# Where weights and first-batch folds of a Fourier + two-MoE kernel are prepared: ahead of the first step, or within the steps

## The chip, the cores and the metric

One NeuronCore of a Trainium2 chip runs the whole program. The metric is device time in microseconds (us); lower is better. Engines are named TensorE (PE, with its weight loads as PEld), VectorE (DVE), ScalarE (ACT), GpSimd (POOL) and SyncE (SP, which here only issues transfers).

## The reference

```python
X = np.fft.fft(np.fft.fft(x, axis=1), axis=2).real     # x: 8 x 3072 x 256
x = X.reshape(24576, 256)
g = x @ w_gate; val = x @ w_val                        # 256 x 1536 each
x = (g * sigmoid(g) * val) @ w_out                     # 1536 x 256
logits = x @ m2_gate                                   # 256 x 8, routing with capacity 3072 per expert
out[mask_e] = relu(x[mask_e] @ w1[e]) @ w2[e]          # for each expert e
```

The inputs are float32, except the three weights of the first MoE: they are float64, and the kernel narrows their 64-bit words to float32 itself.

## The kernel before

The program has two phases. `phase1` computes the real part of the 2-D FFT and the first MoE; `phase2` routes tokens and runs the second MoE. The change is in `phase1` only.

**Tiles and steps.** `phase1` works on 48 tiles of 512 tokens (6 tiles for each of 8 batches). A tile has 12 steps, one for each 128 columns of the hidden layer (`NF` = 12), so there are 576 steps `g`. One step does, in this order of the program (lines 674 to 702): `advance(2g)`, the side work of slot A(g); `products(g, 1)` into bank Q, which ScalarE copies to `qs`; `products(g, 0)` into a bank Pp; ScalarE's rounding `hi` and GpSimd's remainder `lo` of step g-2; `columns(g)`, four VectorE operations; ScalarE's Silu and VectorE's `hidden(g-1)`; `out_proj(g-3)`, 12 TensorE products into four Y banks; `advance(2g+1)`, the side work of slot Z(g). The order is written out by hand: an engine runs its instructions in the order of the program, and waits where one needs another engine's result.

**Side work.** `at(s, gen)` puts a generator into slot s. Every `advance` takes one piece (up to the next `yield`) from each generator in its slot and moves it on to the next slot, so a generator with four pieces runs through four half-steps.

**What is prepared.** The transform along the 3072 axis uses cosine and sine tables on TensorE; before it, `fold` adds and subtracts the four mirrored parts of an x tile (five elementwise operations) into `z0` to `z5`, six folds for a batch. The transform along 256 is folded into the weights: `narrow` turns 64-bit words into float32 on VectorE (four operations, and one ScalarE mask), and `fold_w` multiplies a 512-column block of w_gate or w_val by the cd or sd table on TensorE, from where ScalarE takes the rounded part, and for sd also a row that goes to HBM and comes back as `w2`, and VectorE the remainder (line 214). There are three blocks `j`, each good for four steps of a tile: block 0 for columns 0 to 3, and so on. `prep_wo(c)` narrows two row blocks of w_out, transposes them on TensorE (line 240), rounds them (ScalarE line 243, GpSimd line 244), and multiplies the transposed blocks with `m2g` (line 248), which gives the eight logit columns that `prep_wl` appends to all six pairs (lines 254, 255). `fft_t` transforms column 128 for all batches in six parts; its result goes to HBM (`tscr`) and comes back, broadcast, as `tb`, one row for each tile. `fft_half` transforms a tile, sine and cosine half; it needs `tb`, the ce and se tables, and all six `z`.

**The start of phase 1** (lines 518 to 629) is straight code up to step 0. All loads go through SP's queue in the order written: W block 0, cd and sd, the column-128 data, m2g, x tiles 0 and 1, w_out in two groups with x tiles 2 and 3 in between, x tile 4, later x tile 5, ce, se, W blocks 1 and 2. VectorE narrows block 0; folds 0, 2, 4 run on GpSimd and 1, 3, 5 on VectorE; the six `prep_wo` are interleaved with them, using Y banks; then come the column-128 part, the two half transforms of tile 0, and the narrowing of block 1. Within the steps, `prep_units(1)` starts in slot Z(0), `prep_block(2)` in A(1), with bank F (one buffer) for block 2's products. The later parts for column 128 and tile 1's half transforms use bank F as well.

Of the kernel before, what the change touches and what calls it, by code (L numbers as in the profile page):

```python
# [86 lines left out]
def phase1(ctx, tc, io, yscr, Lall, ident, idt, NT, choice=None):  # L87
# [142 lines left out]
    def prep_wo(c, pl):  # L230
# [6 lines left out]
        pp = bank("Y", 4).rearrange("p (c t f) -> p c t f", c=2, t=2)  # L237
# [7 lines left out]
        yield  # L245
        for i in range(2):
            for t in range(2):
                nc.tensor.matmul(pl[:, E * (c + i) : E * (c + i) + E], woT[:, i, t, :], m2g[:, t, :], start=(t == 0), stop=(t == 1))
        yield

    def prep_wl(pl):
        for j, w in Wo.items():
            v = pl[:, 2 * E * j : 2 * E * j + 2 * E].rearrange("p (c e) -> p c e", c=2)
            nc.scalar.copy(w[:, :, 0, D:EXT], v)
            nc.vector.tensor_sub(w[:, :, 1, D:EXT], v, w[:, :, 0, D:EXT].bitcast(F32))
# [276 lines left out]
    load_x0(0)  # L532
    load_x0(1)
    for c in (0, 2, 4):
        load_wo(c)
    load_x0(2)
    load_x0(3)
    for c in (6, 8, 10):
        load_wo(c)
    load_x0(4)  # L540
    sp0 = fold_special(0, nc.vector, (("z5", 2), ("z4", 2)))
    next(sp0)

    for gv in range(2):
        narrow_w(0, gv)
    fw = [fold_w(0, gv, cs, "Y", 4) for gv in range(2) for cs in range(2)]
    for x in fw:
        next(x)
    vt = (("hi", 3), ("lo", 3))
    pl = bank("Pp", 2)  # L550
    pw = [prep_wo(c, pl) for c in range(0, NF, 2)]
    run(fold(0, 0, x0[0], nc.gpsimd), fold(0, 1, x0[1], nc.vector, vt))
    next(pw[0])
    for x in fw[0:2]:
        next(x)
    next(pw[1])
    for x in fw[2:4]:
        next(x)
    next(pw[0])
    x0.append(load_x(0, 5))  # L560
    load_tab("ce")
    load_tab("se")
    load_w(1)
    load_w(2)
    fold_t(xt, tsp)
    fp = [fold(0, i, x0[i], nc.gpsimd) for i in (2, 4)]
    fv = [fold(0, i, x0[i], nc.vector, vt) for i in (3, 5)]
    f2 = iter([x for i in (0, 1) for _ in range(10) for x in (fp[i], fv[i])])

    def some(n):  # L570
        for _ in range(n):
            next(next(f2))

    tt = fft_t(0, 0)
    for k in range(2, 8):
        some(8 if k < 7 else 0)
        if k < 6:
            next(pw[k])
        if k < 7:
            next(pw[k - 1])  # L580
        next(pw[k - 2])
        if k == 3:
            next(tt)
# [726 lines left out]
```

## Time and profile before

| | before |
|---|---|
| time, median of 3 (lowest, highest) | 3226.61 us (3226.33, 3227.45) |
| profiled execution, own time | 3226.93 us |
| its span | 3225.2 us |
| TensorE busy | 3100.4 us (96%) |
| VectorE busy | 2568.9 us (80%) |
| GpSimd busy | 1642.6 us (51%) |
| ScalarE busy | 1530.9 us (47%) |
| HBM read, written | 88.67 MB, 51.18 MB |

Busy time is the union of an engine's instructions; "xN" merges N alike instructions in a row. The granted clock (PEclk) is TensorE's, as a part of 2.4 GHz. "idle ... <-" names what ended an engine's idle time before an instruction.

### The profile page before, as it was taken

How to read it: one execution, taken by the hardware profiler on the slowest of the kernel's cores; microseconds unless marked ns; L12 is line 12 of the kernel's file. 1: busy time of each engine (PE TensorE's matmuls, PEld its weight loads, DVE VectorE, ACT ScalarE, POOL GpSimd, SP SyncE). 2: the span in 40 equal slices, each digit the busy share in tenths (PEclk: the TensorE clock that was granted, in tenths of full speed). 3: DMA queues.
4: the chain of work that ended last, by engine and by line, in shares of the span. 5: the costliest groups of instructions: out<-in, count | busy, mean ns of one | idle time of the engine just before them, and what ended most of it. 6: DMA issues, size and time to landing. Idle time of an engine off the chain costs nothing. (4 is left out here: it accounts for less than half of the span.)

```text
span 3225.2 us, 63210 instructions
## 1 busy us (share of the span) xinstructions
PE 3100.4 (96%) x23835; PEld 2927.4 (91%) x23835; DVE 2568.9 (80%) x5678; ACT 1530.9 (47%) x3034; POOL 1642.6 (51%) x1761
## 2 busy tenths in 40 slices
PE   6999999999999999999999985989999999999998
PEld 4899999999999999999999984868888888888998
DVE  8899999999999999999998887776767676765322
ACT  3555565565555555555565552233333333333332
POOL 3474674664764855846744443343434343434442
PEclk7999999999999999999999996989999999999999
DMA  5110100100100101101000001112121212112111
GB/s 208 31 38 20 44 31 32 44 25 24 51 20 31 51 18 38 38 18 46 31 25 11 18 34 43 42 61 68 41 69 42 69 42 73 41 67 70 51 44 37
DMA packets 71441, 143.94 MB, mean 45 GB/s; under 512 B 13602, under 2 KB 47442, under 8 KB 69088
## 3 DMA queue, kind: packets, MB, share of 16 engines
q1 hardware_dynamic: 50388, 71.96, 6.8%
q0 software_dynamic: 20736, 67.92, 6.4%
q8 instruction: 189, 3.10, 0.4%
q14 instruction: 116, 0.95, 0.1%
q10 hardware_dynamic: 12, 0.01, 0.0%
HBM read 88.67 MB, written 51.18 MB: 43 GB/s over the span
## 5 line engine op out<-in xcount | busy, mean ns | idle before, releaser
L688 POOL TENSOR_TENSOR lo<-hh,hi 128x512 fp32r<-128x512 f32 x576 | 745.2, 1294 | 752.4 <-ACT hi L687 739.6
L412 PE MATMUL Y<-Wo,hi 128*128 128x264 f32 x4608 | 866.5, 285 | 0.1
L412 PEld LDWEIGHTS Y<-Wo,hi 128*128 128x128 f32 x4608 | 710.2, 188 | 0.3 <-ACT hi L687 0.3
L412 PE MATMUL Y<-Wo,lo 128*128 128x264 f32 x2304 | 654.6, 284 | 5.2 <-POOL lo L688 5.2
L681 ACT COPY qs<-Q 128x512 f32<-128x512 f32 x576 | 340.0, 590 | 520.7 <-PE Q L381 511.0
L392 DVE SCALAR_TENSOR_TENSOR T<-tb,w,Q 128x256 f32<-128x256 f32 x1152 | 500.5, 475 | 97.9 <-ACT qs L681 91.3
L1141 PE MATMUL B<-w,hh 128*128 128x256 f32 x3072 | 577.2, 287 | 0.2 <-ACT hh L1121 0.2
L1150 POOL DMA_INDIRECT out_dram<-ot,id x192 | 192.5, 1003 | 585.1 <-ACT ot L1148 453.8
L1115 PE MATMUL A<-yh,w 128*128 128x512 f32 x1536 | 490.2, 400 | 0.1
L1141 PEld LDWEIGHTS B<-w,hh 128*128 128x128 f32 x3072 | 473.7, 189 | 3.3 <-ACT hh L1121 0.3
L400 DVE TENSOR_TENSOR hh<-sl,G 128x512 f32<-128x512 f32 x576 | 475.3, 825 | 1.1 <-issue 1.1
L381 PE MATMUL Q<-xh,W 128*128 128x256 f32 x2304 | 446.3, 286 | 14.4 <-DVE T L392 7.9
L412 PEld LDWEIGHTS Y<-Wo,lo 128*128 128x128 f32 x2304 | 434.1, 188 | 7.6 <-POOL lo L688 7.6
L1141 PE MATMUL B<-w,hl 128*128 128x256 f32 x1536 | 431.7, 281 | 0.2 <-DVE hl L1132 0.2
L381 PE MATMUL Pp<-xh,W 128*128 128x256 f32 x2304 | 431.2, 280 | 0.0
L687 ACT CAST hi<-hh 128x512 fp32r<-128x512 f32 x576 | 360.5, 626 | 70.8 <-DVE hh L400 66.1
L1132 DVE SCALAR_TENSOR_TENSOR hl<-A,hh 128x512 fp32r<-128x512 f32 x384 | 263.2, 687 | 163.4 <-ACT hh L1121 140.8
L393 DVE TENSOR_TENSOR G<-Pp,qs 128x512 f32<-128x512 f32 x576 | 392.2, 681 | 0.0
L394 DVE TENSOR_TENSOR G<-T,Pp 128x512 f32<-128x512 f32 x576 | 389.0, 675 | 0.0
L381 PEld LDWEIGHTS Q<-xh,W 128*128 128x128 f32 x2304 | 353.4, 188 | 27.1 <-ACT hi L687 14.4
L1121 ACT ACTIVATE hh<-A 128x512 fp32r<-128x512 f32 x384 | 229.3, 597 | 309.1 <-PE A L1115 256.5
L695 ACT ACTIVATE sl<-G 128x512 f32<-128x512 f32 x576 | 365.3, 634 | 0.0
(252 smaller groups left out, 5100.5 us busy)
## 6 DMA issues: line engine op xcount, KB each, us to landing
xs<-in_x_dram SPq DMA_DIRECT2D x43, 512.0 KB
yscr<-ys SPq DMA_DIRECT2D x40, 528.0 KB
tb<-tscr SPq DMA_DIRECT2D x48, 128.0 KB
raw<-in_wg_dram SPq DMA_DIRECT2D x6, 512.0 KB
raw<-in_wv_dram SPq DMA_DIRECT2D x6, 512.0 KB
rawWo<-in_wo_dram SPq DMA_DIRECT2D x12, 256.0 KB
yg<-yscr,idx POOLq DMA_INDIRECT x192
out_dram<-ot,id POOLq DMA_INDIRECT x192
```

The costliest lines, as they stand in the source:

```text
L381: nc.tensor.matmul(pp[:, gv * 256 : gv * 256 + 256], W[:, cs, gv, a, cc : cc + P], RI[t][cs][d], start=(i == 0), stop=(i == 2))
L392: nc.vector.scalar_tensor_tensor(T[:, gv, :], tb, w2[:, gv, c : c + 1], pq[:, gv * 256 : gv * 256 + 256], op0=ALU.mult, op1=ALU.add)
L393: nc.vector.tensor_sub(G[:, 0, :], pp, qs)
L394: nc.vector.tensor_add(rev(G[:, 1, :])[:, :, ::-1], T, rev(pp))
L400: nc.vector.tensor_mul(hh, s["sl"], s["G"][:, :, 256:512])
L412: nc.tensor.matmul(Yp[t][u], h[a][:, u * P : (u + 1) * P], Wo[c // 2][:, c % 2, d, :], start=(c == 0 and i == 0), stop=(c == NF - 1 and i ...
L681: nc.scalar.copy(s["qs"], s["pq"])
L687: nc.scalar.copy(hi, s["hh"])
L688: nc.gpsimd.tensor_sub(lo, s["hh"], hi.bitcast(F32))
L695: nc.scalar.activation(s["sl"], s["G"][:, :, 0:256], AF.Silu)
L1115: nc.tensor.matmul(pa, w[:, a, c : c + P], res["y", i][d][:, k, :], start=(n == 0), stop=(n == 5))
L1141: nc.tensor.matmul(pb[:, 0:D], h[a][:, s * P : (s + 1) * P], w[:, d, (f % 2) * D : (f % 2) * D + D], start=(n == 0), stop=(n == 23))
```

## The change

Four things. Loads: x tiles 0 to 5 come ahead of ce and se, and w_out and W blocks 1 and 2 behind them; x tile 5 is staged in the `ys` buffer. Ahead of step 0 only W block 0 is prepared, and all six folds run on VectorE. `prep_wo` takes bank F for its transposes and for its logit product, and appends its own pair's logit columns; `prep_wl` is gone. Block 1's narrowing goes into slots Z(0) and A(1), block 2 starts in A(2), and w_out pair c in A(c + 1), c = 0, 2, ..., 10.

```diff
-    def prep_wo(c, pl):
+    def prep_wo(c):
...
-        pp = bank("Y", 4).rearrange("p (c t f) -> p c t f", c=2, t=2)
+        pp = bank("F", 1).rearrange("p (c t f) -> p c t f", c=2, t=2)
...
         yield
+        pl = bank("F", 1)
         for i in range(2):
             for t in range(2):
-                nc.tensor.matmul(pl[:, E * (c + i) : E * (c + i) + E], woT[:, i, t, :], m2g[:, t, :], start=(t == 0), stop=(t == 1))
-        yield
-
-    def prep_wl(pl):
-        for j, w in Wo.items():
...
+                nc.tensor.matmul(pl[:, E * i : E * i + E], woT[:, i, t, :], m2g[:, t, :], start=(t == 0), stop=(t == 1))
+        yield
+        v = pl[:, 0 : 2 * E].rearrange("p (c e) -> p c e", c=2)
+        nc.scalar.copy(w[:, :, 0, D:EXT], v)
+        nc.vector.tensor_sub(w[:, :, 1, D:EXT], v, w[:, :, 0, D:EXT].bitcast(F32))
+        yield
...
-    load_x0(0)
-    load_x0(1)
-    for c in (0, 2, 4):
-        load_wo(c)
...
+    for i in range(5):
+        load_x0(i)
     sp0 = fold_special(0, nc.vector, (("z5", 2), ("z4", 2)))
     next(sp0)
+    x0.append(work.tile([P, 4, EXT], F32, tag="ys", bufs=1, name="x0")[:, :, 0:D])
+    nc.sync.dma_start(x0[5], io["x"][0, 5].rearrange("p (m d) -> p m d", m=4))
+    load_tab("ce")
+    load_tab("se")
+    load_wo(0)
+    load_w(1)
+    for c in range(2, NF, 2):
+        load_wo(c)
+    load_w(2)
 
     for gv in range(2):
         narrow_w(0, gv)
+    fold_t(xt, tsp)
     fw = [fold_w(0, gv, cs, "Y", 4) for gv in range(2) for cs in range(2)]
+    tt = fft_t(0, 0)
     for x in fw:
         next(x)
...
+    for x in fw:
         next(x)
...
-    for k in range(2, 8):
-        some(8 if k < 7 else 0)
...
+    for i in range(6):
+        run(fold(0, i, x0[i], nc.vector))
+        if i == 2:
             next(tt)
-        if k == 4:
+        if i == 3:
             next(tt)
             load_w2(0)
             tb0, r0 = load_tb(0), {}
...
-    prep_wl(pl)
...
-    narrow_w(1, 0)
     RI[0] = (r0[False], r0[True], tb0)
-    narrow_w(1, 1)
...
-    def prep_block(j):
+    def prep_block(j, *banks):
 
         for gv in range(2):
             narrow_w(j, gv)
             yield
-            if gv == 0:
+            if gv == 0 and j == 2:
                 yield
-        yield from prep_units(j, "F", 1)
+        yield from prep_units(j, *banks)
...
-    at(Z(0), prep_units(1, "Y", 4))
-    at(A(1), prep_block(2))
+    at(Z(0), prep_block(1, "Y", 4))
+    at(A(2), prep_block(2, "F", 1))
+    for c in range(0, NF, 2):
+        at(A(c + 1), prep_wo(c))
```

## Rows read from the trace of the kernel before

**Rows 1.** Busy time by stretch: stretch and length, busy (instructions) per engine, PEclk, DMA share, GB/s.

```profile
5.87:63.39 57.52, 34.28 (x129) 26.08 (x129) 48.83 (x83) 18.37 (x40) 26.70 (x22) 0.67 0.77 276
63.39:129.92 66.53, 58.41 (x362) 47.01 (x363) 58.26 (x112) 33.88 (x63) 14.92 (x13) 0.92 0.08 16
30.00:60.00 30.00, 19.64 (x92) 18.02 (x92) 24.21 (x42) 7.93 (x20) 15.94 (x13) 0.50 0.68 245
200.00:400.00 200.00, 198.92 (x1664) 197.82 (x1663) 185.97 (x352) 118.49 (x233) 119.15 (x109) 1.00 0.09 29
```

**Rows 2.** Timeline of TensorE, steps 0 and 13: start, duration, instruction, idle before it.

```profile
63.39 0.50 PE L381 MATMUL Q<-xh,W 128*128 128x256 f32 x2 [1.80 <-ACT xh L366]
...
129.92 0.39 PE L381 MATMUL Q<-xh,W 128*128 128x256 f32 x2
```

**Rows 3.** Timeline of VectorE: folds and narrowings of w_out ahead of step 0.

```profile
15.37 0.68 DVE L120 TENSOR_TENSOR fa<-x 128x512 f32<-128x512 f32 x1
...
22.50 0.69 DVE L178 SCALAR_TENSOR_TENSOR wo<-wm,wo 128x512 f32<-128x512 f32 x1
...
35.70 0.42 DVE L127 TENSOR_TENSOR fb<-fa 128x256 f32<-128x256 f32 x1
36.15 0.42 DVE L131 TENSOR_TENSOR z<-fb 128x256 f32<-128x256 f32 x1
36.74 0.43 DVE L172 TENSOR_SCALAR wo<-rawWo 128x512 int32<-128x512 int32 x1 [0.17 <-issue]
...
38.73 1.57 DVE L178 SCALAR_TENSOR_TENSOR wo<-wm,wo 128x512 f32<-128x512 f32 x1
```

**Rows 4.** Timeline: the last weight product of block 0 and a ScalarE read.

```profile
18.82 1.88 PE L207 MATMUL Y<-wt,sd 128*128 128x512 f32 x4
...
21.21 0.58 ACT L212 ACTIVATE row<-Y 1x512 f32<-1x512 f32 x1
```

**Rows 5.** Timeline: first half transform's weight loads, and VectorE's use of tb.

```profile
56.06 1.41 PEld L321 LDWEIGHTS Y<-ce,z 128*128 128x128 f32 x6
...
62.61 0.28 DVE L362 TENSOR_SCALAR ab<-tb 1x256 f32<-1x256 f32 x1
```

**Rows 6.** Busy time by stretch, at the end of the bulk and behind it.

```profile
43.00:44.00 1.00, 1.00 (x6) 1.00 (x6) 0.93 (x3) 1.00 (x4) 0.05 (x1) 0.50 0.63 254
...
49.00:51.00 2.00, 0.04 (x1) 0.00 (x0) 1.86 (x3) 0.00 (x0) 2.00 (x2) 0.50 0.47 71
```

**Rows 7.** Timeline: issues of SP's queue, and GpSimd's first fold, which waited for x.

```profile
9.77 0.82 SPq L531 DMA_DIRECT2D x<-in_x_dram  x2
...
13.42 3.77 POOL L120 TENSOR_TENSOR fa<-x 128x512 f32<-128x512 f32 x1 [11.86 <-DMA x<-in_x_dram]
...
46.83 0.29 SPq L294 DMA_DIRECT2D tscr<-tt  x1
...
48.54 0.44 SPq L336 DMA_DIRECT2D tb<-tscr  x1
```

**Rows 8.** Timeline of VectorE: narrowing of block 1 (two halves), and columns of step 0.

```profile
63.71 0.76 DVE L172 TENSOR_SCALAR wt<-raw 128x512 int32<-128x512 int32 x2
...
72.46 0.87 DVE L392 SCALAR_TENSOR_TENSOR T<-tb,w,Q 128x256 f32<-128x256 f32 x2
...
73.85 0.68 DVE L394 TENSOR_TENSOR G<-T,Pp 128x512 f32<-128x512 f32 x1
```

**Rows 9.** Timeline: TensorE's preparation work, and a weight remainder on VectorE.

```profile
35.93 1.09 PE L240 MATMUL Y<-ident,wo 128*128 128x128 f32 x4 [5.20 <-DVE wo L178]
36.81 1.72 PE L248 MATMUL Pp<-m2g,woT 128*128 128x8 f32 x8
...
67.62 3.73 PE L207 MATMUL Y<-wt,cd 128*128 128x512 f32 x4 [1.68 <-DVE wt L178]
...
74.31 0.38 PE L326 MATMUL F<-alt,tz 128*8 128x128 f32 x2
...
107.87 0.69 DVE L214 TENSOR_TENSOR W<-F,W 128x512 fp32r<-128x512 f32 x1 [1.69 <-ACT row L212]
```

More of the change, by code (lines that the diff above doesn't have):

```diff
@@ L245, in prep_wo @@
         yield
+        pl = bank("F", 1)
         for i in range(2):
             for t in range(2):
-                nc.tensor.matmul(pl[:, E * (c + i) : E * (c + i) + E], woT[:, i, t, :], m2g[:, t, :], start=(t == 0), stop=(t == 1))
+                nc.tensor.matmul(pl[:, E * i : E * i + E], woT[:, i, t, :], m2g[:, t, :], start=(t == 0), stop=(t == 1))
         yield
-    def prep_wl(pl):
-        for j, w in Wo.items():
-            v = pl[:, 2 * E * j : 2 * E * j + 2 * E].rearrange("p (c e) -> p c e", c=2)
-            nc.scalar.copy(w[:, :, 0, D:EXT], v)
-            nc.vector.tensor_sub(w[:, :, 1, D:EXT], v, w[:, :, 0, D:EXT].bitcast(F32))
+        v = pl[:, 0 : 2 * E].rearrange("p (c e) -> p c e", c=2)
+        nc.scalar.copy(w[:, :, 0, D:EXT], v)
+        nc.vector.tensor_sub(w[:, :, 1, D:EXT], v, w[:, :, 0, D:EXT].bitcast(F32))
+        yield
     tscr = dram.tile([B, 6 * 256], F32, name="tscr")
@@ L531, in phase1 @@
     load_x0 = lambda i: nc.sync.dma_start(x0[i].rearrange("p m d -> p (m d)"), io["x"][0, i])
-    load_x0(0)
-    load_x0(1)
-    for c in (0, 2, 4):
-        load_wo(c)
[L536 to L540, printed above, removed]
+    for i in range(5):
+        load_x0(i)
     sp0 = fold_special(0, nc.vector, (("z5", 2), ("z4", 2)))
     next(sp0)
+    x0.append(work.tile([P, 4, EXT], F32, tag="ys", bufs=1, name="x0")[:, :, 0:D])
[7 more added lines that the diff above has]
+    load_w(2)
     for gv in range(2):
         narrow_w(0, gv)
+    fold_t(xt, tsp)
     fw = [fold_w(0, gv, cs, "Y", 4) for gv in range(2) for cs in range(2)]
+    tt = fft_t(0, 0)
     for x in fw:
         next(x)
[L549 to L554, printed above, removed]
-        next(x)
[L556 to L574, printed above, removed]
-    for k in range(2, 8):
-        some(8 if k < 7 else 0)
[L577 to L582, printed above, removed]
+    for x in fw:
+        next(x)
+    for i in range(6):
+        run(fold(0, i, x0[i], nc.vector))
+        if i == 2:
             next(tt)
-        if k == 4:
+        if i == 3:
             next(tt)
```

## The prediction

> **What bounds the kernel now.** I read the table of busy time by stretch first. Between 200 and 400 us TensorE is busy 198.92 of 200 us and VectorE 186 [rows 1]: there each step costs what TensorE needs, and a delay ahead of it is carried to the end, because all later TensorE work is the same. At the start it is VectorE that is nearly full: 48.83 of 57.52 us from the first weights to step 0, 58.26 of 66.53 us from there to step 13 (88%) [rows 1]. So the question is when the kernel gets past its preparation, and I compare the start of one step in both kernels. Read on the timeline, step 0 starts (first Q product) at 63.39 and step 13, behind the last of the six w_out pairs, at 129.92 [rows 2]. Engines take their instructions in program order, so the rest is a replay of the new order on VectorE, TensorE and ScalarE with the durations of the old trace.
>
> **The change part by part.**
>
> *Ahead of step 0.* Narrowing W block 0 is unmoved: VectorE ends it at 15.4, where its first fold starts now [rows 3]. Then come the small folds for column 128, the four subtractions of the split W block 0, and all six folds. The last of the four weight products ends on TensorE at 18.82 + 1.88 = 20.7, two ScalarE reads of 0.6 follow to 21.8 (second row of the group) [rows 4], so the last subtraction ends at 22.5. A fold undisturbed by GpSimd is one add of 0.68 (first row) and four that follow each other at 0.45 (35.70 to 36.15), 2.5 us [rows 3]; six are 15 us: 37.5. The column-128 result and the special row, six VectorE operations of 0.15 to 0.4 us, bring it to 39.1 (1.6, an estimate). That removes from this stage six narrowings, six sets of transposes and 12 small copies. GpSimd's three folds go to VectorE for 7.5 us; the three that VectorE has now are stretched beside GpSimd (about 13 us by their starts and ends), so this costs it only some 2 us.
>
> The half transforms then run on TensorE at 39.1 as they do at 56.06 now; that is 63.39 − 56.06 = 7.33 us to the first product, with VectorE's multiply of tb 0.78 us ahead of it [rows 2, 5]. Without a wait step 0 starts at 46.4. But tb is read back from HBM by a transfer that is now issued behind all 14.9 MB of the preparation (x 3.1, W 6.3, w_out 3.1, tables and small ones 2.4), by a write of tscr on the same queue. In the old trace these bytes end within the stretch 43 to 44, at 63% of the engines [rows 6]; their number is the same, so I keep 43.65. Today the write of tscr is issued at 46.83, tb's read at 48.54, and its data moves until about 50.9: 4.1 us (from 49 to 51 us 142 KB moved, and tb has 131) [rows 6, 7]. From 43.65 that gives 47.7, and 0.8 later step 0 at **48.5**. The bounds are 46.4 (the small write passes the bulk) and 49.5 (the last bulk transfers land 1 us late); I take 48.5, because transfers of this queue land in the order of issue where it can be seen: the x tile issued at 9.77 was there at 13.42 [rows 7], when some 3.6 MB had moved, which is what had been issued up to it.
>
> The Trainium skill, in "DMA: Bandwidth & Descriptors", section "Queues, rings and completion order", says that each DMA engine takes the descriptors of one queue in ring order. It speaks against the change; by it step 0 is at 48.5 and the total 3250, without it 46.4 and 3248. No row shows a small transfer behind so much bulk.
>
> *Steps 0 to 3.* VectorE's queue after step 0 starts (times from then): columns(0) done at 4.0; narrowing block 1 twice, 2 × 4.37 (72.46 − 63.71 for two) [rows 8]; the evacuation of the second column-128 product 0.55; w_out pair 0, four operations, 2.7 (36.74 to 38.73 plus an undisturbed 0.69) [rows 3]; columns(1) and hidden(0), 2.75 (72.46 to 73.85, and two times 0.68) [rows 8]: 18.75. Next in the queue is the evacuation of the third column-128 product. TensorE could start what leads to it only when pair 0 was narrowed (16.0): transposes 1.1, two weight products, 3.73 behind a pause and 1.88 in full flow, together 5.45 as the pause is half over, and the product itself, which ends at 74.69 after 1.7 [rows 4, 9]; with ScalarE's 0.3 that is 24.6. VectorE waits 5.85 us; behind it in its queue stand the subtractions of block 1 and all of step 2, and TensorE and ScalarE wait for those. (The mask of a narrowing shares two buffers with qs; that wait is over before VectorE comes to columns, so it costs nothing.) Then 0.55 + 1.45 + 4.4 (block 2, first half) + 2.75 + 1.55 + 4.35 (second half) + 2.7 (pair 1): pair 1 is narrowed 42.4 us after step 0, at **90.9**.
>
> *Steps 4 to 7.* Here pairs 1 and 2 and the four weight products of block 2 share the one F bank, and each use is released by a VectorE subtraction in its queue. From the end of a narrowing (0): transposes and copy to 1.8 while VectorE does columns and hidden to 2.75; weight product 1.9, ScalarE 0.6, subtraction 0.7: 5.0; the small products with m2g 0.9; products of the step up to Q 0.75, copy 0.6, columns and hidden 2.75: 10.0; the logit columns' evacuation 0.25; the next weight product 1.9, two ScalarE reads 1.25, subtraction 0.7 (it waits for the row copy, as 107.87 shows [rows 9]), next narrowing 2.7: about 16.8. VectorE works 11 of these. Of TensorE's prices the low-clock ones (transposes 1.1 for 4, m2g products 1.72 for 8, a weight product 3.73 [rows 9]) hold only in the first of two such rounds, since TensorE stood idle for over 6 us ahead of it: 17.9 + 16.1 = **34.0**, pair 3 narrowed at 124.9.
>
> *Steps 8 to 12.* Pairs 4 and 5 and tile 1's two half transforms go through F in the same way. Columns and hidden of steps 7 and 8 with the logit evacuation, until the half transform may write, 6.4; its products 1.35 and evacuation 1.2; narrowing pair 4, 2.7; columns and hidden of step 9, 2.75; the other half's evacuation 1.0; m2g products 0.9, step 10's Q 0.75, copy 0.6, columns and hidden 2.75, evacuation 0.2; narrowing pair 5, 2.7; transposes and copy 1.25, m2g products 0.9, TensorE's 2.9 of step 12: **28.3**, step 13 at 153.2.
>
> Sum: step 0 is 63.4 − 48.5 = 14.9 us earlier, and from step 0 to 13 it takes 42.4 + 34.0 + 28.3 = 104.7 instead of 66.5, 38.2 more. Net +23.3. The profiled execution took 3226.93 (span 3225.2 and 1.7 around it; 0.3 above the median of 3226.61), so **3250**.
>
> What hides nothing any more: w_out's 6 × 2.7 of VectorE (16.2) had the wait for data and the half transforms' tables beside it before; now TensorE waits for it. GpSimd's subtraction and ScalarE's copies of w_out I cost at nothing: both engines are free for more than half of each step there; if GpSimd's cover is gone, out_proj waits 1.3 us per pair.
>
> One price has far bounds: a narrowing beside GpSimd. The last of its operations takes 0.69 alone (22.50) and 1.57 beside one (38.73) [rows 3], so the six cost from 0 to 6 × 0.9 × 2 = 11 us more. I take 0, since GpSimd's 1.3 us per step mostly falls on columns, whose inputs lie in PSUM. The Trainium skill, in "GPSIMD Engine Reference", section "1. Specifications", says that GpSimd shares its SBUF interfaces with VectorE and gets in the way of instructions with two SBUF inputs. The row at 38.73 agrees; it speaks for the folds' move and against the narrowings beside the steps, and by it the total is 3250 to 3261.
>
> **The rivals.**
> 1. *VectorE stays as full as it is now.* From step 0 to 13 its work grows from 58.26 by w_out's 16.2 and six small subtractions to 75.5 us. At 88% busy, as now, that takes 85.8, step 13 comes at 134.3, +4.4: 3231; at 95% it takes 79.5 and the total is 3225; with step 0 at 46.4 as well, and 4 us saved on narrowings that GpSimd's folds stretch now, 3219. For it: weight products and half transforms slide under VectorE's queue now. Against it: the single F bank and two evacuations queued ahead of columns put TensorE and VectorE in series; my sum has it 72% busy. It decides from about 87% on. This is the case of not slower.
> 2. *The bank's chain is shorter.* If transposes, weight products and m2g products overlap the columns of the step in front, a round of two steps is VectorE's 11 to 13 us rather than 16.8: 8 us less in steps 4 to 7 and 4 in steps 8 to 12, 3238.
> 3. *The clock stays low.* If TensorE's waits keep it at the lower level through step 8, three more weight products at 3.73, two sets of transposes and the steps' products cost 10 to 15 more: 3263. For it: from 30 to 60 us, where TensorE waits for data again and again, the granted clock is 0.5, the lower of its levels [rows 1]. Against it: in steps 4 to 7 TensorE works 11 of 17 us.
>
> **How the numbers follow.** Forecast 0.62 (its own range 3240 to 3258: ten waits on the bank 1 us shorter each, or the narrowings stretched by two thirds of their bound), rival 1 0.15 (0.06 of it faster, 0.09 no change), rival 2 0.13, rival 3 0.10. No change means within 0.2%, 6.5 us. Slower is then 0.62 + 0.13 + 0.10 = 0.85. The range leaves out rival 1 and the upper half of rival 3: 3234 to 3262.
>
> **What would show it.** Right: the first Q product at 46 to 50 us; VectorE waiting for the third column-128 product for 4 to 7 us; in steps 4 to 7 VectorE idle 2 to 3 us ahead of each weight subtraction and TensorE waiting for narrowings; step 13 at 148 to 160; equal step pace from there. Wrong: step 13 before 137; a first product later than 52, which would be the transfers; or TensorE no longer at 99% after 200 us.

## The result and the profile after

The changed kernel takes **3271.46 us** (median of 4 runs, 3268.0 to 3272.79), the kernel before 3226.55 beside it (4 runs, 3226.33 to 3227.45): ratio **1.0138**, interval 1.0123 to 1.0153. It is slower, as forecast, but by 45 us and not by 23; 3271 lies above the range of 3234 to 3262. The profiled execution took 3268.0 (span 3266.2), the lowest of the four; the steps below are compared with that.

Busy time by stretch in the changed kernel (stretch and length, busy and instructions of PE, PEld, DVE, ACT, POOL, then PEclk, DMA share, GB/s). The first two rows and the last answer to [rows 1]:

```profile
5.87:52.04 46.17, 18.38 (x57) 10.43 (x57) 27.98 (x68) 7.43 (x15) 0.00 (x0) 0.75 0.89 317
52.04:166.16 114.12, 80.93 (x434) 64.75 (x435) 76.14 (x141) 44.45 (x87) 25.82 (x19) 0.80 0.08 23
...
20.00:30.00 10.00, 3.15 (x14) 1.41 (x14) 8.70 (x20) 1.25 (x3) 0.00 (x0) 0.75 0.76 242
46.00:47.00 1.00, 0.00 (x0) 0.00 (x0) 0.00 (x0) 0.00 (x0) 0.00 (x0) 0.50 0.48 54
90.00:100.00 10.00, 4.52 (x8) 1.90 (x8) 7.07 (x11) 3.40 (x6) 2.90 (x2) 0.50 0.00 0
150.00:160.00 10.00, 9.13 (x49) 9.16 (x50) 5.45 (x12) 3.79 (x9) 2.15 (x3) 0.59 0.00 0
...
200.00:400.00 200.00, 199.38 (x1662) 198.00 (x1661) 184.79 (x352) 118.20 (x233) 119.23 (x109) 1.00 0.11 32
```

Step 0 starts at 52.04 (before: 63.39) and step 13 at 166.16 (before: 129.92): 11.35 us earlier, but the stretch from step 0 to step 13 is 47.6 us longer (114.12 for 66.53). From 200 us on TensorE is as full as it was. VectorE's work up to step 13 did not grow: 27.98 + 76.14 = 104.1 us, where the kernel before has 48.83 + 58.26 = 107.1 [rows 1]. What grew is the time in which VectorE does nothing: 17.0 us before (124.05 − 107.1), 56.2 now (160.29 − 104.1). The whole loss up to step 13 is waits of VectorE. (Both sums run from 5.87, where VectorE's first instruction of the kernel before starts.)

Timeline of TensorE in the changed kernel (start, duration, instruction, idle before it and what ended that); the first and the last row answer to [rows 2], the two between are the same kind of weight product at two clocks:

```profile
52.04 0.80 PE L380 MATMUL Q<-xh,W 128*128 128x256 f32 x2 [12.49 <-ACT xh L365]
...
96.56 3.77 PE L207 MATMUL F<-wt,cd 128*128 128x512 f32 x4 [0.67 <-ACT woT L242]
...
115.77 1.98 PE L207 MATMUL F<-wt,cd 128*128 128x512 f32 x4 [0.67 <-ACT woT L242]
...
166.16 0.40 PE L380 MATMUL Q<-xh,W 128*128 128x256 f32 x2
```

Timeline of VectorE in the changed kernel, the waits on the way (the bracket is the idle time ahead of the instruction) and the last operation of three narrowings, of pairs 0, 1 and 3:

```profile
51.27 0.28 DVE L361 TENSOR_SCALAR ab<-tb 1x256 f32<-1x256 f32 x1 [10.72 <-DMA tb<-tscr]
...
67.29 0.69 DVE L178 SCALAR_TENSOR_TENSOR wo<-wm,wo 128x512 f32<-128x512 f32 x1
...
76.45 0.28 DVE L289 TENSOR_TENSOR tt<-F,tod 8x128 f32<-8x128 f32 x1 [5.89 <-ACT tod L287]
...
93.09 1.56 DVE L178 SCALAR_TENSOR_TENSOR wo<-wm,wo 128x512 f32<-128x512 f32 x1
...
100.99 0.69 DVE L214 TENSOR_TENSOR W<-F,W 128x512 fp32r<-128x512 f32 x1 [3.75 <-ACT W L209]
...
104.25 0.87 DVE L391 SCALAR_TENSOR_TENSOR T<-tb,w,Q 128x256 f32<-128x256 f32 x2 [2.57 <-ACT qs L654]
...
110.24 0.69 DVE L214 TENSOR_TENSOR W<-F,W 128x512 fp32r<-128x512 f32 x1 [3.23 <-ACT row L212]
...
130.46 1.56 DVE L178 SCALAR_TENSOR_TENSOR wo<-wm,wo 128x512 f32<-128x512 f32 x1
...
154.86 0.87 DVE L391 SCALAR_TENSOR_TENSOR T<-tb,w,Q 128x256 f32<-128x256 f32 x2 [4.13 <-ACT qs L654]
```

The same waits of 52 to 166 us in sums (waiting tile and line, what it waited for: us in total, times, longest us):

```profile
DVE T L391 <- ACT qs L654: 15.0, 6, 4.1
DVE W L214 <- ACT row L212: 6.7, 3, 3.2
DVE tt L289 <- ACT tod L287: 5.9, 1, 5.9
DVE W L214 <- ACT W L209: 5.2, 2, 3.7
```

Timeline of SP's queue in the changed kernel: the bulk loads, then the small write and the read of tb that hang on it:

```profile
14.77 8.45 SPq L107 DMA_DIRECT2D ce<-in_ce_dram  x6
...
27.98 9.51 SPq L228 DMA_DIRECT2D rawWo<-in_wo_dram  x10
...
40.55 0.30 SPq L293 DMA_DIRECT2D tscr<-tt  x1
...
47.76 0.34 SPq L335 DMA_DIRECT2D tb<-tscr  x1
```

The forecast's terms beside what the profile has (each from the starts and ends of instructions; pair 1 is narrowed at 93.09 + 1.56 = 94.65, pair 3 at 130.46 + 1.56 = 132.02):

| term | forecast | profile | off by |
|---|---|---|---|
| start of step 0 | 48.5 | 52.04 | +3.5 |
| step 0 to pair 1 narrowed | 42.4 | 42.6 | +0.2 |
| two rounds to pair 3 narrowed | 34.0 | 37.4 | +3.4 |
| from there to step 13 | 28.3 | 34.1 | +5.8 |
| start of step 14 to start of step 575 (561 steps), against 1777.53 before | 0 | +4.66 | +4.7 |

"Steps 14 to 575" stands below for the stretch of that last row. The column of differences is 17.6 us, and 3250 + 17.6 comes within half a microsecond of the profiled execution's 3268. The median lies another 3.5 us above that execution.

### The profile page after: what moved, and what is told of

It reads as the page before. It is cut to its first block, busy times and chain, and to the rows that moved or that the text cites. A ratio compares the mean times of both kernels' runs of the same rounds, so it can differ in the third digit from the quotient of the medians.

```text
span 3266.2 us, 63173 instructions
## 1 busy us (share of the span) xinstructions
PE 3113.2 (95%) x23835; PEld 2936.9 (90%) x23835; DVE 2563.4 (78%) x5693; ACT 1529.3 (47%) x3034; POOL 1632.0 (50%) x1746
```

## The experiments

Theory after the result: four separate terms were mis-sized, tb's wait, the chain through bank F, the clock, and the pace of the later steps. Rivals: the prepared work itself is what costs (folds, narrowings on VectorE), or the terms are one chain, in which what is saved at one place is waited for at the next. The kernels of e1 to e4, e6, e8 and e9 start from the changed kernel, the others from the kernel before. A step's start is read from one profiled execution of each kernel, and the four runs of the changed kernel lie 4.8 us apart, so differences of a few us between such starts can be chance.

**e1: the bulk behind tb's read.** The ten loads of w_out pairs 1 to 5 and the four of W block 2 are issued after the read of tb.

```diff
-    for c in range(2, NF, 2):
-        load_wo(c)
-    load_w(2)
...
             tb0, r0 = load_tb(0), {}
+            for c in range(2, NF, 2):
+                load_wo(c)
+            load_w(2)
```

> The changed kernel with the loads of w_out pairs 1 to 5 and of W block 2 issued behind tb's read instead of ahead of it. In the changed kernel VectorE stood 10.7 us in front of its use of tb. Theory 1 (part of the loss is tb waiting behind the bulk on one queue): step 0 starts at 41 to 43 us instead of 52.0, and as every later step hangs on VectorE and TensorE, the gain is carried to the end: about 3261 us. Theory 2 (the early steps are held by something other than their start, such as the landing of the weights or the side work's slots): step 0 is early, step 13 stays near 166, total 3268 to 3272.

3262.53 us (3261.64 to 3263.36), 1.011 of the kernel before (1.0093 to 1.0127). Step 0 starts at 41.51, 10.5 earlier than in the changed kernel; step 13 at 159.27, 6.9 earlier. The time and step 0 are what theory 1 had (about 3261, and 41 to 43). VectorE's use of tb in this kernel:

```profile
40.74 0.28 DVE L361 TENSOR_SCALAR ab<-tb 1x256 f32<-1x256 f32 x1 [0.17 <-DMA tb<-tscr]
```

The wait of 10.72 us is gone, so it came from the transfers queued ahead, and nothing else stood behind it. But 3.6 us of it were given back in steps 5 and 6, where TensorE now runs at half its clock for most of the time (mean granted clock 0.68 from 100 to 110 us): timeline of TensorE in this kernel, to be set against the row of 115.77 above:

```profile
104.05 1.12 PE L240 MATMUL F<-ident,wo 128*128 128x128 f32 x4 [2.48 <-DVE wo L178]
105.84 3.78 PE L207 MATMUL F<-wt,cd 128*128 128x512 f32 x4 [0.68 <-ACT woT L242]
```

**e2: the m2g product in a bank of its own.** It takes a Pp buffer, and no longer waits for bank F.

```diff
-        pl = bank("F", 1)
+        pl = bank("Pp", 2)
```

> The changed kernel with one word changed: the small product of w_out with m2g goes into a Pp bank instead of F, so that F is shared by transposes and weight products alone. No work is removed. Theory 1 (the one F bank, released by subtractions in VectorE's queue, puts the engines in series): rounds of two steps get 3 to 4 us shorter in steps 4 to 7, 2 to 4 us are saved in steps 8 to 12, step 13 at about 155 instead of 166, total about 3261. Theory 2 (it is VectorE's added work, whatever the bank): no change, 3269 to 3273.

3263.41 us (3261.36 to 3264.53), ratio 1.011 (1.0094 to 1.0127). Step 0 at 52.85 (0.8 later than in the changed kernel), step 4 at 101.50 (1.2 earlier), step 8 at 130.24 (4.1 earlier), step 11 at 147.60 (10.3 earlier), step 13 at 161.05 (5.1 earlier). The theory had step 13 at about 155, so the effect is about half of what was expected. The sharing of bank F is part of the price of these steps. The narrowing of pair 5 starts 8.6 us earlier than in the changed kernel (149.34 for 157.95), but 3.6 of these are lost behind it: 1.0 because it now falls beside a GpSimd operation (it takes 3.62 us instead of 2.67), 0.8 in the m2g products at the low clock (1.88 us instead of 1.06), 1.9 in step 12, which takes 4.91 us for 2.98. Busy time of e2 in step 12:

```profile
156.14:161.05 4.91, 4.91 (x25) 4.91 (x26) 2.63 (x6) 1.69 (x4) 1.81 (x2) 0.55 0.29 112
```

**e3 and e4: w_out pairs put back ahead of step 0,** three of them or all six, with their transposes in Y banks as before the change, and their m2g products in Y banks too (before the change these went into a Pp bank). `prep_wo` takes its bank as an argument for this, and only the remaining pairs go into slots. The remarks behind # give e4's values.

```diff
...
     next(fr)
+    pw = [prep_wo(c, "Y", 4) for c in range(0, 6, 2)]      # e4: range(0, 12, 2)
+    for k in range(3 + 3):                                  # e4: 6 + 3
+        for s in range(4):
+            if 0 <= k - s < 3:
+                next(pw[k - s])
     next(fi)
```

> The changed kernel with w_out pairs 0, 1 and 2 prepared ahead of step 0 (in Y banks), while VectorE waits for tb anyway; pairs 3, 4, 5 stay in the steps. Theory 1 (bank chain): besides 3 times 2.7 us of narrowing the two rounds of steps 4 to 7 lose most of their waits: about 20 us less, 3250. Theory 2 (VectorE's work alone): 8 us less, 3263.

> The changed kernel with all six w_out pairs prepared ahead of step 0; folds on VectorE, load order and block 1 in the steps stay changed. VectorE's 16 us of narrowing stand in its wait of 10.7 us for tb, so step 0 at about 58. Theory 1 (what costs is w_out within the steps): from there 66 us to step 13 as in the kernel before, step 13 at about 124, total 3221 to 3229. Theory 2 (VectorE's work alone): 10.7 us less than the changed kernel, about 3260. Theory 3 (folds on VectorE or the load order carry much of the loss): between these, above 3240, with a late step 0.

e3: 3244.78 us (3243.74 to 3248.4), ratio 1.0058 (1.0042 to 1.0075); step 0 at 55.87, step 13 at 140.68. e4: 3235.84 us (3233.72 to 3237.04, 8 runs), ratio 1.0028 (1.0018 to 1.0039); step 0 at 64.59, step 13 at 130.42. e3 is 5 us better than the first theory's 3250. Three pairs ahead cost step 0 3.8 us and bring step 13 25.5 us nearer; the other three cost 8.7 and bring 10.3. In e4 step 13 is where it was before the change (129.92), with folds, loads and block 1 still as changed: moving w_out into the steps is what makes step 13 late. The theory's figures for e4 were missed all the same: it had step 0 at 58, step 13 at 124 and 3221 to 3229 us. e4 is 9 us slower than the kernel before, its profiled execution 7.0 us (3233.97 and 3226.93). Most of that lies behind step 13: steps 14 to 575 take 1782.98 us, in the kernel before 1777.53.

**e5 and e6: the same instructions at other places in SBUF.** The tiles of SBUF get their places in the order in which they are first asked for, and the change altered that order. e5 is the kernel before with every tile where the changed kernel has it, e6 the changed kernel with the places of the kernel before. One line for each pool, ahead of the first load, asks for the tiles in the other kernel's order:

```diff
+    for n in ['W0', 'Wo0', 'W1', 'Wo1', 'Wo2', 'Wo3', 'Wo4', 'Wo5', 'W2']:
+        const.tile(..., tag=n, bufs=1, name="place")
+    for n in ['tb', 'tsp', 'G', 'z5', 'ys', 'xs', 'qs', 'lo', 'fa', 'fb', 'z0', ..., 'T', 'hh', 'sl', 'hi']:
+        work.tile(..., tag=n, bufs=shape[n][1], name="place")
```

> The kernel before, with its SBUF tiles and weight tiles placed at the addresses that they have in the changed kernel; order of the instructions and everything else untouched. The changed kernel's steps 14 to 575 took 1782.2 us in its profile, the kernel before's 1777.5, though they run the same code. Theory (the placement in SBUF sets the pace of the steps): step 13 stays at 130, steps 14 to 575 take 1782, total about 3231. Rival (the pace comes from something else, such as what stands ahead of these steps in the program, or varies by itself): steps 14 to 575 take 1777.5 and the total stays at 3226 to 3227.

> The changed kernel, with its SBUF tiles and weight tiles placed at the addresses that they have in the kernel before; order of the instructions untouched. Theory (the placement sets the pace): step 13 stays at 166, steps 14 to 575 take 1777.5 instead of 1782.2, total about 3266. Rival (not the placement): 1782 and 3268 to 3272.

| kernel | step 13 | steps 14 to 575 | time, us (runs) | ratio to before |
|---|---|---|---|---|
| before | 129.92 | 1777.53 | 3227.77 (19) | |
| e5: before, places of after | 128.48 | 1783.48 | 3232.53 (10) | 1.0018 (1.0009 to 1.0028) |
| after | 166.16 | 1782.19 | 3271.46 (4) | 1.0138 (1.0123 to 1.0153) |
| e6: after, places of before | 170.37 | 1777.37 | 3266.35 (4) | 1.0123 (1.0106 to 1.0139) |

The pace goes with the places in both directions, 4.8 and 6.0 us over 561 steps, about 10 ns each. The other traces agree: 1782.06 to 1783.45 in e1 to e4 and e8, which have the changed kernel's order, 1777.39 to 1777.60 in e7, e9, e10 and e11, which have the old one. One thing did not come as expected: step 13 of e6 stays not at 166 but comes at 170.37, though its instructions are those of the changed kernel. That is one execution, and not explained; its median of four runs is 5.1 us below the changed kernel's. Busy time between 600 and 1800 us in the kernel before, then in e5 (columns as above):

```profile
600.00:1800.00 1200.00, 1192.54 (x9924) 1183.41 (x9923) 1110.30 (x2102) 704.38 (x1389) 731.36 (x677) 1.00 0.10 31
```

```profile
600.00:1800.00 1200.00, 1192.95 (x9889) 1184.09 (x9888) 1107.21 (x2094) 701.55 (x1385) 730.97 (x675) 1.00 0.10 31
```

TensorE is as full in both, at full clock, and gets 35 products fewer done (9889 for 9924, 0.35%): by the busy time each takes a trifle longer (120.6 ns for 120.2), and none waits for anything that the profile names.

**e7: the folds on VectorE, alone,** in the kernel before.

```diff
-    run(fold(0, 0, x0[0], nc.gpsimd), fold(0, 1, x0[1], nc.vector, vt))
+    run(fold(0, 0, x0[0], nc.vector), fold(0, 1, x0[1], nc.vector, vt))
...
-    fp = [fold(0, i, x0[i], nc.gpsimd) for i in (2, 4)]
+    fp = [fold(0, i, x0[i], nc.vector) for i in (2, 4)]
```

> One part of the change alone: in the kernel before, the even folds of the first batch go to VectorE instead of GpSimd; the weights stay where they were. Theory (VectorE's work ahead of step 13 is what counts, and this adds to it): step 13 some 2 us later than 129.9, total 3228 to 3230. Rival one (VectorE has room while it waits for the first transfers, or its narrowings get shorter with GpSimd idle beside them): 3224 to 3227. Rival two (this part is a large share of the 36 us lost): step 13 at 140 or later, 3237 or more.

3224.71 us (3222.97 to 3225.95, 10 runs), ratio 0.9991 (0.9982 to 1.0001), step 13 at 127.44: no slower; the 3 us between the medians are not clear of noise. Busy time of the kernel e7 from the first weights to step 13:

```profile
5.87:60.88 55.01, 32.62 (x129) 25.37 (x129) 46.66 (x98) 18.22 (x40) 10.25 (x7) 0.69 0.81 288
60.88:127.44 66.56, 58.42 (x362) 47.03 (x363) 58.29 (x112) 33.85 (x63) 14.91 (x13) 0.92 0.08 16
```

VectorE does 15 instructions more ahead of step 0 than before (98 for 83) in 2.2 us less of busy time (46.66 for 48.83 [rows 1]): what it takes over costs less than what GpSimd's folds had added to VectorE's own instructions. The first rival held (3224 to 3227).

**e8: TensorE kept at work.** Three 128x512 products whose result nobody reads stand ahead of the transposes of pairs 1 to 5 in the changed kernel, in bank F (`flatw` is 512 columns of the table ce).

```diff
...
         pp = bank("F", 1)
+        if c:
+            for _ in range(3):
+                nc.tensor.matmul(pp, tab["cd"][:, 0, :], flatw, start=True, stop=True)
```

> The changed kernel, with three products of 128x512 added ahead of the transposes of each w_out pair from 1 to 5, into the bank that those transposes then write; their result is never read. They only keep TensorE at work while it waits. In the changed kernel four float32 transposes took 3.77 us where the clock was low and 1.98 us where it was full. Theory (the low clock costs the chain of transposes, narrowing and next transposes several us in steps 4 to 12): the clock stays full, transposes take 2.0 us, step 13 comes 4 to 8 us earlier than 166.2, total 3264 to 3267. Rival (the added products stand in the chain themselves and the clock costs less than they do): step 13 at 166 to 172, total 3271 to 3276.

(The 3.77 and 1.98 us in this text are the weight products of line 207 shown above, not transposes.) 3267.94 us (3267.83 to 3269.16), ratio 1.013 (1.0113 to 1.0147). Step 13 at 164.50, 1.7 us earlier: less than the theory's 4 to 8, and not later, as the rival had it. The stretches of e8 that answer to the two of the changed kernel above:

```profile
90.00:100.00 10.00, 4.51 (x8) 1.88 (x8) 6.51 (x11) 3.98 (x7) 2.96 (x2) 0.66 0.00 0
150.00:160.00 10.00, 9.58 (x63) 7.67 (x62) 7.86 (x14) 4.36 (x10) 3.54 (x3) 1.00 0.01 2
```

Between 150 and 160 us the granted clock is 1.00 (2.4 GHz) instead of 0.59, and step 10 takes 2.97 us instead of 5.35. At 90 to 100, where TensorE had stood idle again, the added products did not lift it enough. The narrowing of pair 5 starts 2.9 us earlier than in the changed kernel (155.07 for 157.95), so that much was won by then. Of it 1.0 us is lost at once, as in e2, because the narrowing now falls beside a GpSimd operation. Timelines of VectorE and GpSimd in e8:

```profile
156.24 1.65 DVE L176 SCALAR_TENSOR_TENSOR wo<-rawWo,wo 128x512 int32<-128x512 int32 x1
```

```profile
155.79 1.55 POOL L667 TENSOR_TENSOR lo<-hh,hi 128x512 fp32r<-128x512 f32 x1 [1.28 <-ACT hi L666]
```

The added products are in the way too: they still ran when pairs 4 and 5 were narrowed, so the transposes started 0.6 us behind the narrowing each time. So the 1.7 us are a net figure, and what the clock alone costs was not isolated by a run.

**e9: three terms out at once,** the edits of e1, e2 and e6 together.

> The changed kernel with three of the terms that the forecast missed taken out at once: the loads of w_out pairs 1 to 5 and of the last weight block issued behind tb's read (step 0 at 41 instead of 52), the m2g product in a bank of its own (step 13 came 5 us earlier by that alone), and the tiles at the addresses of the kernel before (steps 14 to 575 in 1777.4 instead of 1782.2). Alone they gave 8.9, 8.1 and 5.1 us against the changed kernel's 3271.46. Theory (they are separate terms and add up): step 13 at 153 to 155, steps 14 to 575 in 1777.5, total 3248 to 3251. Rival (the first two relieve the same chain of VectorE waits, and what the one gives the other can't give again): step 13 at 157 to 160, total 3254 to 3258.

3247.28 us (5 runs, 3244.94 to 3253.85), ratio 1.006 (1.0046 to 1.0074); step 13 at 150.47, steps 14 to 575 in 1777.39. 24.2 us under the changed kernel, where the three alone had given 8.9 + 8.1 + 5.1 = 22.1. In time they add up, within the noise. In the traces they do more than that: step 13 came 6.9 and 5.1 us earlier in e1 and e2 and 4.2 later in e6, which would put it at 158.4, and it is at 150.47. Why is not known; the traces are of one execution each. The rival, that the terms take the same waits (3254 to 3258), is out. Busy time of e9 from the first weights to step 13:

```profile
5.87:42.80 36.93, 20.06 (x56) 11.19 (x56) 27.97 (x68) 7.44 (x15) 0.00 (x0) 0.77 0.82 280
42.80:150.47 107.67, 78.82 (x434) 63.72 (x435) 78.36 (x144) 44.56 (x87) 26.49 (x19) 0.83 0.19 64
```

VectorE does nothing for 36.93 − 27.97 + 107.67 − 78.36 = 38.3 us of this, still 21 more than in the kernel before. No run divides these further; e4 shows that nearly all of the lost time up to step 13 is gone when w_out is not inside the steps.

**e10: block 1 in the slots, alone.** In the kernel before, W block 1 is narrowed in Z(0) and A(1), and block 2 starts in A(2).

```diff
-    narrow_w(1, 0)
     RI[0] = (r0[False], r0[True], tb0)
-    narrow_w(1, 1)
...
-    at(Z(0), prep_units(1, "Y", 4))
-    at(A(1), prep_block(2))
+    at(Z(0), prep_block(1, "Y", 4))
+    at(A(2), prep_block(2, "F", 1))
```

> Another part of the change alone, in the kernel before: weight block 1 is narrowed in the slots of steps 0 and 1 instead of ahead of step 0's products in VectorE's queue, and block 2 from step 2 on; w_out and the folds stay where they were. Theory (VectorE is busy 88% of steps 0 to 13 in the kernel before, so that the order of its work hardly matters): step 13 at 129 to 132, total 3226 to 3229. Rival (starting steps 0 to 3 early, then narrowing within them, makes the steps wait as it does in the changed kernel): step 13 at 135 or later, 3232 or more.

3226.67 us (11 runs, 3224.46 to 3230.27), ratio 0.9996 (0.9987 to 1.0006), step 13 at 127.08: no difference in time that is clear of noise. This part of the change is free where the steps have only it to carry.

**e11: work put into VectorE's waits.** The kernel of e7, and a quarter of block 1's narrowing where VectorE waits for the last m2g products and the first transform; the last pair's products stand behind the transform's on TensorE.

```diff
...
     next(fr)
-    prep_wl(pl)
+    narrow_t(1, 0, 0)
     next(fi)
+    next(pw[5])
     next(fr)
     next(fi)
     run(fr, fi)
-    narrow_w(1, 0)
+    prep_wl(pl)
+    narrow_t(1, 0, 1)
```

(`narrow_t(j, gv, t)` is one half of `narrow_w(j, gv)`; `prep_wl` does its six copies first and its six subtractions behind them. Not shown: the folds' lines as in e7, and the place where the last pair's products stood.)

> The kernel before with the even folds on VectorE (3224.71 by itself) and one more thing: half of the narrowing of the first half of weight block 1 (3.3 us of VectorE) is put where VectorE waits 2.4 us for the last m2g products and 1.1 and 1.4 us for the first transform, and the last pair's m2g products stand behind the transform's products on TensorE. Theory (what counts up to step 13 is VectorE's busy time plus its waits, wherever they fall): step 0 stays at 60 to 62, step 13 at 123.5 to 125 instead of 127.4, total 3221 to 3223. Rival (step 0's start counts and the waits return later): step 13 at 127 to 129, 3224 to 3227.

**3223.05 us** (11 runs, 3222.02 to 3223.67), ratio **0.9983** (0.9974 to 0.9992): 0.17% faster than the kernel before, with the lowest median here; that it is faster than e7 is not clear of noise, as the intervals overlap. Timeline of VectorE in e11, the filled gap (the narrowing's L172 to L178) and the waits that are left of it:

```profile
52.11 0.41 DVE L172 TENSOR_SCALAR wt<-raw 128x512 int32<-128x512 int32 x1
52.55 1.71 DVE L174 SCALAR_TENSOR_TENSOR wt<-raw,wt 128x512 int32<-128x512 int32 x1
54.29 0.69 DVE L176 SCALAR_TENSOR_TENSOR wt<-raw,wt 128x512 int32<-128x512 int32 x1
55.09 0.69 DVE L178 SCALAR_TENSOR_TENSOR wt<-wm,wt 128x512 f32<-128x512 f32 x1
56.23 0.29 DVE L362 TENSOR_TENSOR ab<-Y,od 128x128 f32<-128x128 f32 x1 [0.45 <-ACT od L358]
...
58.11 0.29 DVE L366 TENSOR_TENSOR ab<-od,F 128x128 f32<-128x128 f32 x1 [1.08 <-ACT od L358]
```

Step 0 starts at 59.53, and step 13 at 124.97, 2.5 us before e7's 127.44. The theory held in the trace (123.5 to 125); the time is at the upper edge of its 3221 to 3223.

**e12, e13, e14: which place sets the pace.** The kernel before with only the weight tiles moved as in e5 (e12), only ys moved ahead of xs (e13), only hi moved behind T (e14).

```diff
+    for n in ['W0', 'Wo0', 'W1', 'Wo1', 'Wo2', 'Wo3', 'Wo4', 'Wo5', 'W2']:          # e12
+    for n in ['tb', 'tsp', 'G', 'z5', 'ys', 'xs', 'qs', 'fa', 'hi', 'fb', ...]:     # e13
+    for n in ['tb', 'tsp', 'G', 'z5', 'xs', 'qs', 'fa', 'fb', 'lo', ..., 'T', 'hi', 'ys']:  # e14
```

> The kernel before with only the weight tiles (three blocks and six w_out pairs) at the places that they have in the changed kernel (weight block 1 ahead of w_out pairs 1 to 5); the tiles of the steps stay where they were. All tiles moved gave 5.8 us more over steps 14 to 575. Theory one (the weights' place does it): steps 14 to 575 in 1782 to 1784, total 3231 to 3233. Theory two (the place of the tiles of the steps, xs, qs, lo, hi, hh, sl, ys, does it): 1777.5, total 3226 to 3228.

> The kernel before with one tile moved in SBUF: ys, the output of the steps, stands ahead of xs as in the changed kernel, and the step tiles from xs to T lie 4.2 KB further on each partition; their order is otherwise as before. Theory one (ys first, or the shift that it gives the others, sets the pace): steps 14 to 575 in 1782 to 1784, total 3231 to 3233. Theory two (another tile's place does it): 1777.5 to 1778, total 3226 to 3228.

> The kernel before with one tile moved in SBUF: hi, the first half of the hidden operand that TensorE loads, stands behind T as in the changed kernel, and what lay behind it moves up by its size. Theory one (hi's place, away from lo, sets the pace): steps 14 to 575 in 1782 to 1784, total 3231 to 3233. Theory two (another tile's place does it): 1777.5 to 1778, total 3226 to 3228. If neither this nor the kernel with ys first is slower, the pace hangs on the whole arrangement, and no single tile of these two.

| kernel | steps 14 to 575 | time, us (11 runs each) | ratio to before |
|---|---|---|---|
| e12: weights | 1777.96 | 3228.94 | 1.0002 (0.9993 to 1.0011) |
| e13: ys ahead of xs | 1778.01 | 3227.8 | 1.0005 (0.9996 to 1.0014) |
| e14: hi behind T | 1777.63 | 3227.1 | 1.0004 (0.9995 to 1.0013) |

None of the three does it; the theory named first fell each time. The 6.0 us of e5 come with all the moves together, and which of them it takes stays open.

## Why the prediction was wrong

The sum over VectorE up to step 13, from its first instruction at 5.87, says in one view where every kernel stands (busy from the tables by stretch, the rest is time in which it did nothing):

| kernel | step 0 | step 13 | VectorE busy | doing nothing |
|---|---|---|---|---|
| before | 63.39 | 129.92 | 107.1 | 17.0 |
| after | 52.04 | 166.16 | 104.1 | 56.2 |
| e1 tb's read ahead of the bulk | 41.51 | 159.27 | 104.1 | 49.3 |
| e2 m2g products in Pp | 52.85 | 161.05 | 106.3 | 48.9 |
| e3 three pairs ahead | 55.87 | 140.68 | 103.5 | 31.4 |
| e4 six pairs ahead | 64.59 | 130.42 | 103.2 | 21.4 |
| e7 folds on VectorE | 60.88 | 127.44 | 105.0 | 16.6 |
| e8 TensorE kept at work | 52.19 | 164.50 | 105.1 | 53.5 |
| e9 e1, e2 and e6 | 42.80 | 150.47 | 106.3 | 38.3 |
| e10 block 1 in slots | 61.85 | 127.08 | 106.7 | 14.5 |
| e11 gaps filled | 59.53 | 124.97 | 106.1 | 13.0 |

**The mechanism was right.** VectorE and TensorE wait for each other through the one bank and through evacuations queued ahead of columns; VectorE is 67% busy after step 0 (76.14 of 114.12), where the prediction had 72% and rival 1 wanted 87% or more. Rival 1 is out. The wait for the third column-128 product was 5.89 us, as forecast (5.85), and the term around it came within 0.2 us, which is partly luck: pair 1's narrowing took 0.9 us more than forecast, and small pieces ahead of it 0.7 less. The preparation of w_out inside the steps is the cost: e4 has step 13 back at 130.42 once it is ahead. What failed are sizes, in the terms that follow. Of the signs that the prediction named for being wrong, one came: a first product later than 52 (52.04), "which would be the transfers"; and step 13 lies outside its 148 to 160.

**Step 0: the term of the bulk was mis-sized.** Its end was kept at 43.65, "their number is the same". It is, but SP's queue was filled otherwise. Between 20 and 30 us the transfers used 0.76 of the engines, and the bulk ended at about 46.5 (the row of 46 to 47 us has 54 GB/s). The same stretch of the kernel before was full (columns as above):

```profile
20.00:30.00 10.00, 3.67 (x16) 2.61 (x14) 9.62 (x16) 3.60 (x8) 4.34 (x5) 0.67 1.00 339
```

From 21 to 23 us almost nothing moved, while SP, at the fourth of six loads of table ce, waited. By the profile it waited for `w2scr<-row`, a small write that ScalarE issues when block 0's weight products are read out. Busy time of the changed kernel in these two microseconds, and the waits of SP's queue from 14 to 24 us in the changed kernel and in the kernel before (us in total, times, longest):

```profile
21.00:22.00 1.00, 0.00 (x0) 0.00 (x0) 0.97 (x2) 0.00 (x0) 0.00 (x0) 1.00 0.05 15
22.00:23.00 1.00, 0.00 (x0) 0.00 (x0) 0.96 (x3) 0.00 (x0) 0.00 (x0) 1.00 0.16 14
```

```profile
SPq L107 <- DMA w2scr<-row: 4.3, 1, 4.3
```

```profile
SPq L228 <- DMA w2scr<-row: 2.7, 1, 2.7
```

The kernel before has the same wait, but the transfers issued ahead of it kept the DMA engines full (1.00 above). At full share the two microseconds would have carried 1.8 us more of transfers, of the 2.9 us by which the bulk ended later; that is an estimate from these rows, and a run without the wait was not made. From the bulk's end the chain ran nearly as forecast: tb's read could be issued at 47.76, and it was there at 51.27. That the small transfers wait for the bulk ahead of them, e1 shows: 10.72 us of waiting, and 0.17 with ten w_out and four W loads behind. The Trainium skill, in "DMA: Bandwidth & Descriptors", section "Queues, rings and completion order", has each DMA engine take a queue's descriptors in ring order; both numbers agree with it.

A second miss of step 0 is hidden by this wait. Without a wait the forecast had step 0 at 46.4; in e1, which has none, it starts at 41.51. The folds follow each other at 2.19 us instead of 2.5 (21.63, 23.82, 26.01 in the changed kernel), the special row ends at 36.20 instead of 39.1, and the half transform's products begin beside the folds instead of behind them. Timeline of TensorE in the changed kernel:

```profile
30.20 0.80 PE L320 MATMUL Y<-ce,z 128*128 128x129 f32 x2 [1.31 <-DVE z L131]
```

So the forecast priced the wait for tb at 2.1 us (46.4 to 48.5) where it was 10.7.

**Steps 4 to 7 and 8 to 12: the narrowing and the low clock priced too low.** First, a narrowing beside GpSimd was taken at 0, with 11 us as its bound. The last operation of the narrowings of pairs 1 to 3 took 1.56 us each instead of 0.69, and another one of pair 4's took 1.65: four times about 0.9, 3.6 us, of which pairs 2 to 4, 2.7 us, lie in these two terms. The timeline of GpSimd in the changed kernel has what ran beside pairs 1 and 3:

```profile
92.47 1.64 POOL L661 TENSOR_TENSOR lo<-hh,hi 128x512 fp32r<-128x512 f32 x1 [7.65 <-ACT hi L660]
...
129.85 1.61 POOL L661 TENSOR_TENSOR lo<-hh,hi 128x512 fp32r<-128x512 f32 x1 [6.13 <-ACT hi L660]
```

It is the subtraction for a step's hidden tile, which the forecast had put beside columns. The narrowing's operation ends 0.55 us after it both times: 94.65 behind 92.47 + 1.64 = 94.11, and 132.02 behind 129.85 + 1.61 = 131.46. In e8 it is 157.89 behind 157.34. Where no GpSimd operation was under way at its start, as in pair 0 (67.29), the same operation takes 0.69. So the price depends on where the GpSimd operation falls: it is up to the rest of that operation. The Trainium skill, in "GPSIMD Engine Reference", section "1. Specifications", tells that GpSimd shares SBUF interfaces with VectorE; these rows and e7 agree.

Second, the sum of steps 4 to 7 has a slip. The pieces that the prediction lists for a round add up to 16.8, and to 18.6 with the first weight product at 3.73 instead of 1.9, as it says of the first round: 35.4 for the two, where it wrote 34.0. Measured, the rounds took 19.7 (94.65 to 114.38) and 17.6 (114.38 to 132.02); without the 0.9 of each narrowing that is 18.9 and 16.8. So the chain through bank F was sized rightly by its pieces, and the theory after the result was wrong to count it among the misses. The 3.4 us of this term are 1.4 of the sum, 1.7 of two narrowings and 0.3 of the rest. What e2 won by taking the m2g product out of bank F is time that the forecast had in its sum.

Third, the clock: **rival 3 was half there.** The forecast kept the low level (1.2 GHz) to the first round. It was granted at 90 to 100 us, as assumed, but came back: the mean granted clock is 0.82, 1.00, 0.83, 0.83, 0.90 and 0.59 in the six stretches of 10 us from 100 to 160, where TensorE was busy with products and transforms after it had waited. The m2g products of pairs 4 and 5, timeline of TensorE in the changed kernel:

```profile
150.87 1.85 PE L249 MATMUL F<-m2g,woT 128*128 128x8 f32 x8 [0.97 <-DVE ab L359]
...
162.26 1.06 PE L249 MATMUL F<-m2g,woT 128*128 128x8 f32 x8 [0.73 <-ACT woT L242]
```

In steps 8 to 12 four groups of products that VectorE then waits for are 0.8 to 0.9 us longer each than rows at the full clock: those into Q of steps 8 and 10, the second half transform, and the m2g products of pair 4. That is an estimate of 3.4 us of the 5.8. Pair 4's narrowing beside GpSimd is another 0.9, and 1.5 are in small pieces. e8 agrees as far as it goes: with the clock at 1.00 the narrowing of pair 5 started 2.9 us earlier. The rival's 10 to 15 us are not in it. What the low clock costs depends on what else is late: in e1 it came to the round of steps 5 and 6 and took back 3.6 us of the 10.5 won at step 0.

**The pace of steps 14 to 575 was taken as equal.** It is 4.7 us slower in the changed kernel, with the same instructions, because tiles are asked for in another order and lie elsewhere in SBUF (e5, e6). The prediction gave no reason for an equal pace beyond the steps' being the same.

That e9 takes 3247.28 us, 2.7 under the forecast, is a coincidence: its step 0 starts 5.7 us ahead of the forecast's, and the m2g bank that it takes out was in the forecast's sum, while the narrowings beside GpSimd and the low clock, which the forecast lacked, are still in it. What stays open: which tiles set the pace, whether the bulk ends at 43.65 without SP's wait for the small write, and the clock's share, which is read from rows and not isolated by a run.

## What to carry over

Add up the busy time of the bounding engine to the point where the kernel becomes bound elsewhere, and its waits beside it: here the first was 103 to 107 us in every kernel, and all the large gains and losses up to that point were waits. Work moved behind the first step is not hidden when the steps have to wait for its results on the way: here six w_out pairs within the steps put step 13 36 us later, the same pairs ahead of step 0 left it where it was, and block 1, moved alone, cost nothing (e10). Work put into a wait that exists is nearly free: 3.7 us of it (52.11 to 55.78 in e11) brought step 13 2.5 us nearer. When tiles are first asked for in another order, compare the steady pace before anything else is explained by it.

## What the runs showed of the hardware

- The same program with its tiles at other places in SBUF ran 561 steps in 1783.5 instead of 1777.5 us, with TensorE as full and at full clock; three partial moves (weights, ys, hi) left it at 1777.6 to 1778.0.
- A small write of 8 KB and the read that follows it waited 10.7 us behind loads on the same queue; issued ahead of most of them they cost VectorE 0.17 us.
- Folds moved from GpSimd to VectorE made VectorE's busy time up to step 0 smaller, 46.66 for 48.83 us, with 15 instructions more.
- A VectorE operation of 0.69 us with two SBUF inputs, started while GpSimd's subtraction ran, ended 0.55 us after the subtraction did (94.65 behind 94.11, 132.02 behind 131.46).
- The same four weight products, behind pair 2's transposes, took 3.78 us at the lower clock (e1) and 1.98 at the full one (changed kernel). The low level came back well after the start: the mean granted clock is 0.59 at 150 to 160 us.
- SP's queue stood 4.3 us, by the profile for a small write of another engine's queue, and the DMA engines were at 0.05 and 0.16 in the two microseconds at its end.
